# Keys in two planes: the second plane of a batch added by an accumulating transfer

## The chip, the cores and the metric

One NeuronCore of one Trainium2 chip. The metric is the device time of one execution in microseconds (us), median over runs; lower is better.

## The reference, cut to what matters

Three stages follow each other: an attention over pooled keys and values, a mixture of experts over its output, and a gated two-layer network. The change touches the first. There are 8 batches of 8 heads with 576 queries of 64 numbers, and the 576 keys are averaged in groups of 8, so 72 pooled keys are left.

```python
def _attn_ref(q, k, v):
    B, H, S, D = q.shape          # 8, 8, 576, 64
    pool = 8
    Sp = S // pool                # 72
    scale = 1.0 / np.sqrt(D)
    k_p = k.reshape(B, H, Sp, pool, D).mean(axis=3)
    v_p = v.reshape(B, H, Sp, pool, D).mean(axis=3)
    scores = scale * np.matmul(q, k_p.transpose(0, 1, 3, 2))
    scores = scores - np.max(scores, axis=-1, keepdims=True)
    attn = np.exp(scores)
    attn = attn / (np.sum(attn, axis=-1, keepdims=True) + 1e-09)
    return np.matmul(attn, v_p)
```

## The kernel before

`attention` runs over 36 tiles of 128 queries, 9 tiles for each two batches (the ninth is half of the one batch and half of the other). Each engine executes its instructions in the order in which the code issues them, except that DMA issues may be placed somewhat ahead of other work of their engine. Iteration i of the loop issues work for three tiles at once:

- `scores(i + 2)`: TensorE multiplies queries and pooled keys (`s<-kbd,q`, two PSUM tiles from the shared pool `hp` of three), VectorE takes the maxima (`mx<-s`), ScalarE the exponentials (`prb<-s,mx`, eight instructions).
- `ptrans(i + 1)`: TensorE transposes the probabilities (`pt<-ident,prb`), ScalarE copies them out of PSUM (`pts<-pt`).
- `pv(i)`: TensorE multiplies them with the pooled values (`pv<-vex,pts`); its PSUM tile has one buffer, so `pv(i + 1)` waits until VectorE's `post(i)` (`sm`, `cc`, `x`, `lg`) has read it.

Behind that, iteration i also prepares the batch b + 1 that comes next, placed by `first[b]`, the first tile of batch b (0, 4, 9, 13, 18, 22, 27, 31). For b from 1 to 6:

- at i = first[b] - 2: `loadq(b + 1)` on SyncE's queue, the first half of `pool_k(b + 1)` on VectorE, `pool_v(b + 1)` on GpSimd (`v<-v` twice, then `vp<-v`), and then `loadk(b + 2)`, `loadv(b + 2)` on SyncE's queue;
- at i = first[b] - 1: the second half of `pool_k(b + 1)`;
- at i = first[b]: `keys(b + 1)`, two ScalarE instructions that scale the pooled keys into `kbd`;
- at i = first[b] + 1: `router1(b + 1)` (TensorE `vtp<-ident,vp`, which needs `vp`) and `values(b + 1)` on GpSimd.

A half of `pool_k` is one VectorE reduction over two of the four head pairs: 128 partitions, 144 outputs, 8 numbers each. The keys of a batch are one transfer of 1152 KB (batch 0: two of 576 KB, one for each half), into a tile with two buffers.

After the ninth tile of a group, `route` appends two steps to a list; the next two iterations pop them. So the iterations i = 9, 18 and 27, which are first[b] for b = 2, 4 and 6, carry ten small VectorE instructions of routing, the iteration behind them about as many more, and GpSimd then issues nine small scatters (`slots<-consts,ix`), two to an iteration.

`raw1` and `raw2` are the landing buffers of the first expert's weights, 16 KB to a partition each; they are written from iteration 25 on.

Of the kernel before, what the change touches and what calls it, by code (L numbers as in the profile page):

```python
# [5 lines left out]
F32 = mybir.dt.float32  # L6
# [7 lines left out]
ALU = mybir.AluOpType  # L14
AX = mybir.AxisListType
# [3 lines left out]
P = 128  # L19
B, H, S, D = 8, 8, 576, 64  # L20
G = 72
# [23 lines left out]
POOL = 8  # L45
# [107 lines left out]
class Kern:  # L153
# [19 lines left out]
    def attention(self, xa, rs, extra):  # L173
        nc, tc, c = self.nc, self.tc, self.c
        self.todo = todo = []
        self.slow = iter(())
        with tc.tile_pool(name="as", bufs=1) as s1, \
# [7 lines left out]
            wr = s1.tile([P, 2, H * (E + 1)], F32, name="wr", tag="wr")  # L185
            mv = c[:, C_MV:C_MV + NINC]
            q_t, k_t, v_t, st = {}, {}, {}, {}

            def loadk(b):
                k_t[b] = s2.tile([P, 4, G, POOL], F32, name=f"k{b}", tag="k")  # L190
                nc.sync.dma_start(k_t[b].rearrange("p a g t -> p a (g t)"), self.kT[b])

            def loadv(b):
                v_t[b] = s2.tile([P, NC, POOL, D], F32, name=f"v{b}", tag="v")
# [3 lines left out]
            def loadq(b):  # L198
                q_t[b] = s2.tile([P, 4, S], F32, name=f"q{b}", tag="q", bufs=3)
                nc.sync.dma_start(q_t[b], self.qT[b])  # L200

            def pool_k(b, eng, halves=(0, 2)):
                k = k_t[b]
                kp = st.get((b, "k"))
                if kp is None:
                    kp = s2.tile([P, 4, G], F32, name=f"kp_{b}", tag="kp")
                if eng is nc.vector:
                    for a in halves:
                        eng.tensor_reduce(kp[:, a:a + 2], k[:, a:a + 2], AX.X, ALU.add)
                else:  # L210
                    eng.tensor_tensor(k[:, :, :, 0:4], k[:, :, :, 0:4], k[:, :, :, 4:8], ALU.add)
                    eng.tensor_tensor(k[:, :, :, 0:2], k[:, :, :, 0:2], k[:, :, :, 2:4], ALU.add)
                    eng.tensor_tensor(kp, k[:, :, :, 0], k[:, :, :, 1], ALU.add)
                st[b, "k"] = kp

            def pool_v(b, on_dve=0):

                v, g, n = v_t.pop(b), nc.gpsimd, on_dve
                vp = st[b, "v"] = s2.tile([P, NC, D], F32, name=f"vp_{b}", tag="vp")
                if n:  # L220
                    nc.vector.tensor_reduce(vp[:CP, 0:n], v[:CP, 0:n].rearrange("p c t d -> p c d t"), AX.X, ALU.add)
                v, vp = v[:CP, n:], vp[:CP, n:]
                g.tensor_tensor(v[:, :, 0:4], v[:, :, 0:4], v[:, :, 4:8], ALU.add)
                g.tensor_tensor(v[:, :, 0:2], v[:, :, 0:2], v[:, :, 2:4], ALU.add)
                g.tensor_tensor(vp, v[:, :, 0], v[:, :, 1], ALU.add)

            def values(b):
                vp, ve = st[b, "v"], vex[b % NB]
                for i, (h0, n) in enumerate(HEADS):
                    j = HOFF[i]  # L230
                    nc.gpsimd.tensor_tensor(ve[:CP, j:j + n, 0:D], bc(vp[:CP, i], 1, n),
                                            bc(mv[:CP, j:j + n], 2, D), ALU.mult)

            def keys(b):
                kp, kb = st.pop((b, "k")), kbd[b % NB]
                for j in range(2):
                    nc.scalar.mul(kb[:, :, j, :], kp, c[:, C_E + j:C_E + j + 1])
# [47 lines left out]
            def scores(t, pss=None):  # L285
                pss = pss or products(t)
                pr = prb[t % 2]
                mx = s2.tile([P, H], F32, name=f"mx_{t}", tag="mx")
                for a, ps in enumerate(pss):
                    nc.vector.tensor_reduce(mx[:, 4 * a:4 * a + 4],  # L290
                                            ps[:, 0:288].rearrange("p (h g) -> p h g", g=G), AX.X, ALU.max,
                                            negate=True)
                    for h in range(4):
                        nc.scalar.activation(pr[:, G * (4 * a + h):G * (4 * a + h + 1)], ps[:, G * h:G * (h + 1)],
                                             AF.Exp, bias=mx[:, 4 * a + h:4 * a + h + 1])
                return pr
# [47 lines left out]
            first = [9 * (b // 2) + 4 * (b % 2) for b in range(B)]  # L344
            one = s1.tile([1, 1], F32, name="one", tag="one")
            self.cb = s1.tile([P, C_N - C_TRI], F32, name="constb", tag="constb")
            nc.vector.memset(one, 0.0)
            k_t[0] = s2.tile([P, 4, G, POOL], F32, name="k0", tag="k")
            for a in (0, 2):
                nc.sync.dma_start(k_t[0][:, a:a + 2].rearrange("p a g t -> p a (g t)"), self.kT[0][:, a:a + 2])  # L350
            nc.scalar.dma_start(self.ident, self.con[:, 0:P])
            nc.scalar.dma_start(c, self.con[:, P:P + C_TRI])
            q_t[0] = s2.tile([P, 4, S], F32, name="q0", tag="q", bufs=3)
# [18 lines left out]
            for i in range(-2, NTILE):  # L372
                if i == -2:
                    pool_v(0, ON0)
                if i + 2 < NTILE and i != -1:
                    prs[i + 2] = scores(i + 2)
                ready = todo.pop(0) if todo and i < NTILE - 1 else None
                if ready and ready[0]:
                    ready[0]()
                if i == -2:  # L380
                    values(0)
                    loadv(1)
                    loadq(1)
                if i == -1:
                    pss = products(1)
                    router1(0)
                if i == 0:
                    pv(0, pts.pop(0))
                if 0 <= i + 1 < NTILE:
                    pts[i + 1] = ptrans(i + 1, prs.pop(i + 1))  # L390
                if i == -1:
                    prs[1] = scores(1, pss)
                    router2(0)
                    pool_k(1, nc.vector, (0,))
                    pool_v(1, ON1)
                    values(1)
                if i > 0:
                    pv(i, pts.pop(i))
                a = ready[1]() if ready and ready[1] else iter(())
                b = post(i) if i >= 0 else iter(())  # L400
                for _ in range(ready[2] if ready and i < NTILE - 2 else 0):
                    next(a, None)
                for _ in b:
                    next(a, None)
                for _ in a:
                    pass
                for _ in range(SLOW):
                    next(self.slow, None)
                if i == 0:
                    pool_k(1, nc.vector, (2,))  # L410
                    keys(1)
                for b in range(B):
                    if i + 2 == first[b]:
                        if 0 < b < B - 1:
                            loadq(b + 1)
                            pool_k(b + 1, nc.vector, (0,))
                            pool_v(b + 1)
                        if b + 2 < B:
                            loadk(b + 2)
                            loadv(b + 2)  # L420
                    if i + 2 == first[b] + 3 + (b == 0) and b + 1 < B:
                        router1(b + 1)
                    if i + 2 == first[b] + 1 and 0 < b < B - 1:
                        pool_k(b + 1, nc.vector, (2,))
                    if i + 2 == first[b] + 2 and 0 < b < B - 1:
                        keys(b + 1)
                    if i + 2 == first[b] + 3 and 0 < b < B - 1:
                        values(b + 1)
                    if i + 2 == first[b] + 5 and b + 1 < B:
                        router2(b + 1)  # L430
                if i == 2:
                    nc.sync.dma_start(self.cb, self.con[:, P + C_TRI:])
                if i == 6:
                    self.consts()
                self.place(2 if i < 27 else 5)
                extra(i)
# [1100 lines left out]
def layout(q, k, v, w_skip, w_gate):  # L1537
    def tr(a):
        return np.ascontiguousarray(a.reshape(B, 4, 2, S, D).transpose(0, 2, 4, 1, 3)).reshape(B, P, 4, S)
    vr = v.reshape(B, H * G, POOL * D)  # L1540
    vr = np.concatenate([vr, np.zeros((B, NC * CP - H * G, POOL * D), v.dtype)], 1)
    vr = vr.reshape(B, NC, CP, POOL * D).transpose(0, 2, 1, 3)
    vr = np.concatenate([vr, np.zeros((B, P - CP, NC, POOL * D), v.dtype)], 1)
    wr = np.concatenate([w_gate, w_skip[:, None]], 1).reshape(H, D, E + 1).transpose(1, 0, 2).reshape(D, H * (E + 1))
    z = np.zeros_like(wr)
    wr = np.ascontiguousarray(np.stack([np.concatenate([wr, z], 0), np.concatenate([z, wr], 0)], 1))
    return tr(q), tr(k), vr, wr


def build(tc, qT, kT, vR, wr, con, w1, w2, w_in, w_out, out):  # L1550
# [55 lines left out]
```

## Time and profile before

| | |
|---|---|
| median of 3 runs | 1301.69 us (1301.1 to 1304.04) |
| the profiled execution's own time | 1305.57 us |
| its span, first to last instruction | 1303.8 us |
| granted TensorE clock, mean over the span | 0.992 |
| busy: PE, DVE, ACT, POOL | 1253.7, 851.5, 576.1, 352.6 us |
| the attention stage | from the start to about 160 us of the span |

PE is TensorE's matmul stream, DVE is VectorE, ACT is ScalarE, POOL is GpSimd, SPq the instructions that SyncE issues to its DMA queue. A number in brackets behind a timeline row is the idle time of that engine just before it and what ended it. Times in the rows are counted from the span's start.

### The profile page before, as it was taken

To read this page: it belongs to the slowest core of one execution; us is meant where nothing else is said; L and a number is where in the kernel's file an instruction comes from. 1 tells how busy PE (TensorE), PEld (TensorE's weight loads), DVE (VectorE), ACT (ScalarE), POOL (GpSimd) and SP (SyncE) were. 2 spreads that over 40 slices of the span, in tenths; PEclk is the share of its full clock that TensorE was granted. 3 is DMA by queue.
4 is the path that set the end of the run, shared out by engine and by line. 5 is a ranking of instruction groups with operands and counts; after the bars stand their busy time and mean duration, and the time that the engine had idled before them with its cause. 6 is when DMAs were issued, how large, how long until landed. Compare 5 with 4: busy or idle time off the path is not lost.

```text
span 1303.8 us, 20308 instructions
## 1 busy us (share of the span) xinstructions
PE 1253.7 (96%) x6469; PEld 1063.6 (82%) x6470; DVE 851.5 (65%) x1557; ACT 576.1 (44%) x1224; POOL 352.6 (27%) x312
## 2 busy tenths in 40 slices
PE   6999797999989999999999999999999999999998
PEld 5888677988888878878888888788888888888887
DVE  5888685676676767879734235556784657847565
ACT  4777534444555445354433344523344343533321
POOL 5466432122222222213457503101111010211100
PEclk9999998999999998999999999999999999999999
DMA  8888446465575632448754322644446353463532
GB/s 343 291 300 284 148 135 212 168 219 189 178 237 185 220 128 91 145 163 269 264 188 183 129 89 103 212 162 137 151 172 218 124 176 111 156 213 118 178 111 91
DMA packets 94187, 234.43 MB, mean 180 GB/s; under 512 B 15077, under 2 KB 26981, under 8 KB 90400
## 3 DMA queue, kind: packets, MB, share of 16 engines
q1 hardware_dynamic: 86816, 216.47, 47.7%
q0 software_dynamic: 7008, 16.80, 4.1%
q8 instruction: 42, 0.69, 0.2%
q14 instruction: 33, 0.27, 0.1%
q10 hardware_dynamic: 288, 0.20, 0.1%
HBM read 183.24 MB, written 52.89 MB: 181 GB/s over the span
## 4 chain that ended last, share of the span: by engine, by line
PE 59%; DVE 2%; DMA 1%; issue 0%; ACT 0%; SPq 0%; DVEq 0%; ACTq 0%
PE yb L110 21%; PE ps L110 17%; PE fh L110 9%; PE fop L110 9%; PE hp L110 2%; PE yp L110 1%; DVE ft L110 1%; PE fxp L110 1%; DVE fr L110 0%; DMA wout<-wdo 0%; PE sx L110 0%; DVE fgl L110 0%; DVE fsg L110 0%; DMA out<-fo 0%; ACT fgh L110 0%
## 5 line engine op out<-in xcount | busy, mean ns | idle before, releaser
L110 PE MATMUL yb<-wout,g 128*128 128x512 f32 x1152 | 268.5, 391 | 0.5 <-DMA wout<-wdo 0.5
L110 PEld LDWEIGHTS yb<-wout,g 128*128 128x128 f32 x1152 | 215.0, 188 | 45.6 <-DMA wout<-wdo 0.7
L110 POOL TENSOR_TENSOR tm<-tm,tm 128x512 f32<-128x512 f32 x24 | 32.2, 1340 | 411.5 <-ACT tm L110 411.5
L110 DVE TENSOR_TENSOR yacc<-yb,yacc 128x512 f32<-128x512 f32 x168 | 115.9, 690 | 38.4 <-PE yb L110 31.2
L110 ACT COPY tm<-ps 128x512 f32<-128x512 f32 x72 | 42.3, 587 | 146.5 <-PE ps L110 144.7
L110 ACT CAST g<-sg 128x512 fp32r<-128x512 f32 x96 | 59.6, 621 | 76.6 <-DVE sg L110 76.6
L110 DVE TENSOR_TENSOR fsg<-fh,fsg 128x512 f32<-128x512 f32 x48 | 33.0, 688 | 81.2 <-ACT fsg L110 81.2
L110 ACT ACTIVATE hh<-hp 128x256 fp32r<-128x256 f32 (+1 forms) x96 | 39.4, 410 | 105.6 <-PE hp L110 96.1
L110 DVE TENSOR_TENSOR w2l<-raw,w2h 128x512 fp32r<-128x512 f32 x96 | 66.1, 693 | 29.2 <-ACT w2h L110 22.2
L110 ACT ACTIVATE prb<-s,mx 128x72 f32<-128x72 f32 x288 | 64.9, 344 | 43.6 <-DVE mx L110 36.7
L110 PE MATMUL yp<-w2h,hh 128*128 128x512 f32 x208 | 83.3, 401 | 0.1
L110 PE MATMUL fh<-w1l,fh 128*128 128x512 f32 x336 | 83.4, 390 | 0.0
L110 PE MATMUL yp<-w2l,hh 128*128 128x512 f32 x208 | 81.2, 390 | 2.1 <-DVE w2l L110 2.1
L110 PE MATMUL hp<-xth,w1h 128*128 128x256 f32 (+2 forms) x384 | 73.3, 314 | 10.2 <-issue 5.9
L110 PE MATMUL yp<-w2h,hl 128*128 128x512 f32 x208 | 81.4, 391 | 0.0
L110 DVE TENSOR_TENSOR tm<-ps,tm 128x512 f32<-128x512 f32 x24 | 16.6, 691 | 98.1 <-PE ps L110 98.1
L110 PE MATMUL hp<-xtl,w1h 128*128 128x256 f32 (+2 forms) x384 | 73.4, 313 | 2.8 <-DVE xtl L110 2.7
L110 PEld LDWEIGHTS fh<-w1l,fh 128*128 128x128 f32 x336 | 62.8, 188 | 12.9
L110 PE MATMUL hp<-xth,w1l 128*128 128x256 f32 (+2 forms) x384 | 71.4, 309 | 0.0
L110 PEld LDWEIGHTS hp<-xth,w1h 128*128 128x128 f32 x384 | 61.4, 195 | 12.1 <-issue 11.0
L110 DVE TENSOR_TENSOR g<-sg,g 128x512 fp32r<-128x512 f32 x96 | 65.7, 685 | 5.4 <-ACT g L110 5.0
L110 ACT ACTIVATE fsg<-fh 128x512 f32<-128x512 f32 x48 | 28.8, 599 | 90.6 <-PE fh L110 90.6
(242 smaller groups left out, 2768.2 us busy)
## 6 DMA issues: line engine op xcount, KB each, us to landing
raw<-w SPq DMA_DIRECT2D x88, 512.0 KB, 3.8
wout<-wdo SPq DMA_DIRECT2D x48, 512.0 KB
win<-wdi SPq DMA_DIRECT2D x36, 512.0 KB
w1l<-wdi SPq DMA_DIRECT2D x36, 512.0 KB
xa<-x SPq DMA_DIRECT2D x36, 256.0 KB
fx<-xa SPq DMA_DIRECT2D x9, 1024.0 KB
v<-vR SPq DMA_DIRECT2D x7, 1280.0 KB
fr<-w_in SPq DMA_DIRECT2D x16, 512.0 KB
```

What stands on the lines that cost most here:

```text
L110: ins = f(*a, **k)
```

## The change

The host lays the keys out in two planes: the first four numbers of every group of eight, and the last four. Batches 0 and 1 load both planes, into `raw1` and `raw2`, and VectorE sums over plane and number at once. From batch 2 on the first plane alone is loaded by SyncE's queue, into a tile of half the size with four buffers; GpSimd then issues a transfer that adds the second plane onto it in SBUF (`addk`), ahead of `pool_v`, and VectorE sums four numbers. Both halves of `pool_k(b + 1)` now stand at i = first[b], just ahead of `keys(b + 1)`.

```diff
             def loadk(b):
-                k_t[b] = s2.tile([P, 4, G, POOL], F32, name=f"k{b}", tag="k")
-                nc.sync.dma_start(k_t[b].rearrange("p a g t -> p a (g t)"), self.kT[b])
+                if b < 2:
+                    raw = (self.raw1, self.raw2)[b].rearrange("p a n -> p (a n)")
+                    k_t[b] = raw[:, 0:POOL * 4 * G].rearrange("p (h a g t) -> p h a g t", h=2, a=4, g=G)
+                else:
+                    k_t[b] = s2.tile([P, 1, 4, G, POOL // 2], F32, name=f"k{b}", tag="k", bufs=4)
+                for h in range(2 if b < 2 else 1):
+                    nc.sync.dma_start(half(b, h), self.kT[b, h])
+
+            def half(b, h=0):
+                return k_t[b][:, h].rearrange("p a g t -> p (a g t)")
+
+            def addk(b):
+                nc.gpsimd.dma_start(half(b), self.kT[b, 1], accum_op=ALU.add)
...
-                if eng is nc.vector:
-                    for a in halves:
-                        eng.tensor_reduce(kp[:, a:a + 2], k[:, a:a + 2], AX.X, ALU.add)
-                else:
...
+                for a in halves:
+                    if b < 2:
+                        eng.tensor_reduce(kp[:, a:a + 2], k[:, :, a:a + 2].rearrange("p h a g t -> p a g h t"), AX.XY,
+                                          ALU.add)
+                    else:
+                        eng.tensor_reduce(kp[:, a:a + 2], k[:, 0, a:a + 2], AX.X, ALU.add)
...
-            k_t[0] = s2.tile([P, 4, G, POOL], F32, name="k0", tag="k")
-            for a in (0, 2):
-                nc.sync.dma_start(k_t[0][:, a:a + 2].rearrange("p a g t -> p a (g t)"), self.kT[0][:, a:a + 2])
+            loadk(0)
...
                     if i + 2 == first[b]:
                         if 0 < b < B - 1:
                             loadq(b + 1)
-                            pool_k(b + 1, nc.vector, (0,))
+                            addk(b + 1)
                             pool_v(b + 1)
...
-                    if i + 2 == first[b] + 1 and 0 < b < B - 1:
-                        pool_k(b + 1, nc.vector, (2,))
                     if i + 2 == first[b] + 2 and 0 < b < B - 1:
+                        pool_k(b + 1, nc.vector)
                         keys(b + 1)
```

## Rows read from the trace of the kernel before

**Rows 1.** The page: busy us of the engines, share of the span, instructions.
```profile
PE 1253.7 (96%) x6469; PEld 1063.6 (82%) x6470; DVE 851.5 (65%) x1557; ACT 576.1 (44%) x1224; POOL 352.6 (27%) x312
```

**Rows 2.** Busy time by stretches of 20 us, the sum of 20 to 140 us.
```profile
sum 120.00, PE 111.68 PEld 100.14 DVE 94.91 ACT 85.71 POOL 76.96; mean PE 18.61 PEld 16.69 DVE 15.82 ACT 14.29 POOL 12.83
```

**Rows 3.** The tile k: its reductions, shortest, median and longest in ns.
```profile
L110 DVE TENSOR_REDUCE kp<-k x16: 1339/1342/1353, 4.8 to 121.4; 128x144 f32<-128x1152 f32 x16
```

**Rows 4.** Timeline (start, length, engine), batch 4 being prepared, 64 to 78 us.
```profile
64.97 1.35 DVE L110 TENSOR_REDUCE kp<-k 128x144 f32<-128x1152 f32 x1
...
66.71 1.80 ACT L110 ACTIVATE prb<-s,mx 128x72 f32<-128x72 f32 x8 [2.04 <-DVE mx L110]
...
67.72 1.60 PE L110 MATMUL s<-kbd,q 128*128 128x144 f32 x8 [0.16 <-ACT prb L110]
...
69.70 1.55 PE L110 MATMUL pv<-vex,pts 120*128 120x148 f32 x10
...
71.09 1.16 PE L110 MATMUL s<-kbd,q 128*128 128x144 f32 x8
...
72.48 0.27 DVE L110 TENSOR_REDUCE lg<-cc 128x9 f32<-128x72 f32 x1
...
72.71 0.76 PE L110 MATMUL pt<-ident,prb 128*120 128x128 f32 x5 [0.46 <-ACT prb L110]
72.75 1.04 ACT L110 ACTIVATE kbd<-kp,consts 128x288 f32<-128x288 f32 x2
...
73.61 1.86 ACT L110 ACTIVATE prb<-s,mx 128x72 f32<-128x72 f32 x8
...
75.10 1.25 PE L110 MATMUL s<-kbd,q 128*64 128x144 f32 x16
...
76.88 1.55 PE L110 MATMUL pv<-vex,pts 120*128 120x148 f32 x10
```

**Rows 5.** Groups of VectorE by form, 20 to 140 us: busy us, mean ns.
```profile
L110 DVE TENSOR_REDUCE mx<-s 128x4 f32<-128x288 f32 x62 | 25.1, 447 | 0.1
```

**Rows 6.** Timeline of the start, 6 to 14 us.
```profile
6.63 1.35 DVE L110 TENSOR_REDUCE kp<-k 128x144 f32<-128x1152 f32 x1 [0.51 <-DMA k<-kT]
...
9.03 2.29 PE L110 MATMUL s<-kbd,q 128*128 128x144 f32 x8 [9.03 <-ACT kbd L110]
9.42 2.78 DVE L110 TENSOR_REDUCE vp<-v 120x192 f32<-120x1536 f32 x1 [1.44 <-DMA v<-vR]
...
13.19 2.29 PE L110 MATMUL s<-kbd,q 128*128 128x144 f32 x8 [1.86 <-DMA q<-qT]
```

**Rows 7.** Timelines of VectorE and TensorE, batch 5 being prepared, 86 to 98 us.
```profile
87.14 1.34 DVE L110 TENSOR_REDUCE kp<-k 128x144 f32<-128x1152 f32 x1
...
92.05 0.82 DVE L110 TENSOR_REDUCE mx<-s 128x4 f32<-128x288 f32 x2
...
92.10 1.63 PE L110 MATMUL pv<-vex,pts 120*128 120x148 f32 x10 [0.23 <-DVE x L110]
...
96.19 1.63 PE L110 MATMUL pv<-vex,pts 120*128 120x148 f32 x10 [0.50 <-DVE sel L110]
```

**Rows 8.** Timelines of GpSimd and TensorE: a direct DMA issue, pooling of batch 4.
```profile
8.78 0.79 POOL L110 DMA_DIRECT2D slots<-table  x1 [0.21 <-POOL x L110]
...
63.43 0.98 POOL L110 DMA_INDIRECT slots<-consts,ix  x1 [0.30 <-issue]
...
72.53 0.87 POOL L110 TENSOR_TENSOR vp<-v 120x320 f32<-120x320 f32 x1
...
74.70 0.47 PE L110 MATMUL vtp<-ident,vp 120*128 120x120 f32 x3
```

**Rows 9.** DMA: GB/s in 40 slices of 20 to 140 us, an issue, a load's landing.
```profile
GB/s 421 431 358 48 313 418 397 322 170 79 323 421 407 283 113 235 381 418 360 188 90 235 421 423 326 186 115 304 422 360 338 133 128 319 352 384 307 350 387 24
...
65.30 0.38 SPq L110 DMA_DIRECT2D q<-qT  x1
...
raw<-w SPq DMA_DIRECT2D x88, 512.0 KB, 3.8
```

More of the change, by code (lines that the diff above doesn't have):

```diff
@@ L206, in pool_k @@
                     kp = s2.tile([P, 4, G], F32, name=f"kp_{b}", tag="kp")
-                if eng is nc.vector:
-                    for a in halves:
-                        eng.tensor_reduce(kp[:, a:a + 2], k[:, a:a + 2], AX.X, ALU.add)
-                else:
-                    eng.tensor_tensor(k[:, :, :, 0:4], k[:, :, :, 0:4], k[:, :, :, 4:8], ALU.add)
-                    eng.tensor_tensor(k[:, :, :, 0:2], k[:, :, :, 0:2], k[:, :, :, 2:4], ALU.add)
-                    eng.tensor_tensor(kp, k[:, :, :, 0], k[:, :, :, 1], ALU.add)
+                for a in halves:
[4 more added lines that the diff above has]
+                        eng.tensor_reduce(kp[:, a:a + 2], k[:, 0, a:a + 2], AX.X, ALU.add)
                 st[b, "k"] = kp
@@ L1543, in layout @@
     vr = np.concatenate([vr, np.zeros((B, P - CP, NC, POOL * D), v.dtype)], 1)
+    kt = np.ascontiguousarray(tr(k).reshape(B, P, 4, G, 2, POOL // 2).transpose(0, 4, 1, 2, 3, 5)).reshape(B, 2, P, -1)
     wr = np.concatenate([w_gate, w_skip[:, None]], 1).reshape(H, D, E + 1).transpose(1, 0, 2).reshape(D, H * (E + 1))
@@ L1546, in layout @@
     wr = np.ascontiguousarray(np.stack([np.concatenate([wr, z], 0), np.concatenate([z, wr], 0)], 1))
-    return tr(q), tr(k), vr, wr
+    return tr(q), kt, vr, wr
 def build(tc, qT, kT, vR, wr, con, w1, w2, w_in, w_out, out):
```

## Prediction

> **What bounds the kernel now.** First the page: TensorE's stream is busy for 96% of the span [rows 1], so work taken from another engine helps only where TensorE stood waiting for it. Then the stretches of the stage that changes: from 20 to 140 us TensorE is busy 111.7 of 120 us, VectorE 94.9, ScalarE 85.7 [rows 2]. All that TensorE could win there is 8.3 us, 0.6% of the kernel. Then the tile k: 16 reductions of 1.34 us [rows 3], 12 of which (batches 2 to 7) the change shortens. Last the timeline around them, for what a reduction holds up; this decides.
>
> Take batch 4. The reduction at 64.97 stands in VectorE's queue ahead of the maxima of tile 14; ScalarE idles 2.04 us for those, its exponentials start at 66.71, and TensorE, which needs their PSUM tiles back, runs its next products in 1.60 instead of about 1.15 us (as at 71.09) after waiting 0.16 [rows 4]. The second one, an iteration later, does the same to tile 15: the transposes at 72.71 had waited 0.46 us [rows 4]. So a reduction of 1.34 us costs TensorE about 0.6 us; it comes twice in each of six batches. That is the prize, about 7 us at most.
>
> **What the reductions become.** The trace has none of 576 elements. Between the row for 288 elements (447 ns) [rows 5] and the one for 1152 (1342 ns) [rows 3] a line gives 447 + 288 x 895/864 = 745 ns. The next instruction starts 1.26 us after a reduction recorded at 1.35 (64.97 to 66.23), so I count 0.66 us each, 1.33 for the pair. Bounds: half of 1342, 0.67, and 576 at the rate of the strided sum over v, 2783 ns for 1536 elements [rows 6], 1.04. On VectorE 12 x (1.26 - 0.66) = 7.2 us go away. But the pair is now issued in one iteration, and directly ahead of keys.
>
> **Batches 2, 4 and 6** (no routing in that iteration), worked on batch 4. Without the early reductions the exponentials of tile 14 start 1.26 earlier, at about 65.5, the products of tile 15 follow the work before them at 67.56, where the wait of 0.16 began, and take 1.15, and pv(13) starts at 69.1 instead of 69.70. The second one gone, the transposes at 72.71 lose their wait too: pv(14) at 72.1 instead of 73.31. So far 1.2 us won. Now the cost: post(13) ended at 72.48 + 0.27 [rows 4] and ends 0.6 earlier, at 72.1; the pair runs until 73.45; keys waits for it on ScalarE and takes 0.95 (before, it ran at 72.75, in front of the exponentials but waiting for nothing [rows 4]); the exponentials of tile 16, queued behind keys, start at 74.4 instead of 73.61. TensorE's products at 75.10 started 1.49 after those, being in need of their PSUM tiles, so now 75.9, and pv(15), 1.78 behind, at 77.7 instead of 76.88 [rows 4]. Two stalls of 0.6 become one of 2.0, because reductions, keys and exponentials now stand in one chain. Net +0.8 us for the batch, +2.4 for three, which repeat the pattern.
>
> **Batches 3, 5 and 7** share that iteration with routing. VectorE has no gap from the reduction at 87.14 to behind the maxima at 92.05, and pv(19) and pv(20) wait for VectorE (0.23 and 0.50) [rows 7]. Taking 1.26 out at 87.14 and putting 1.33 in behind post(18) brings pv(19) from 92.10 to about 90.85, but the maxima at 92.05 come where they came, as does all behind them up to pv(20) at 96.19. Keys pushes the exponentials back 0.5 us, beside VectorE's backlog. I count 0 for the three; bounds -0.6 and +0.5 each.
>
> **The start.** Both planes of batch 0 are needed at once. The second transfer of k was there at 6.63 [rows 6]; both reductions now start there and end at 9.3 instead of 7.98, so the first products move from 9.03 to 10.4 and end at 12.7. The products of tile 1 start at 13.19, waiting for queries [rows 6]: the delay is covered, 0. If summing over two planes ran at the strided rate of v, 2.09 us each, the first products would end at 14.1: +1.0, and +0.6 for batch 1's two reductions at 0.4 of their extra 0.75. So 0 to +1.6; I take 0, since four contiguous numbers are nearer to rows 3 than a stride at every element.
>
> **GpSimd's issue.** A direct issue took 0.79 us [rows 8]. Tightest is batch 4, where pool_v stands behind four scatters: vp ended at 73.40, TensorE read it at 74.70 [rows 8], a slack of 1.3 us. In the new chain TensorE would wait at that place until 75.9 anyway. So 0; an issue beyond 2 us would show there.
>
> **The accumulating transfer** is in no row. VectorE needs it at 72.1 for batch 4. The third of GpSimd's four scatters starts at 63.43 and takes 0.98, with 0.30 before each [rows 8]; the transfer stands behind the second or the fourth, so it is issued at 63.4 or by 66.7. SyncE's queue issues q, k and v from 65.30 on, and such a burst fills the next slices at 381 to 418 GB/s [rows 9]. Lower end: it lands like a plain load of 512 KB, 3.8 us after its issue [rows 9], at 70.5; at 420 GB/s 1.25 of that are bytes and 2.5 are not. Upper end: behind the whole burst (3008 KB) and itself counted twice, since it must read what it adds to: 4.26 MB at 420 GB/s, 10.1 us, and 2.5: 79.3, 7.2 late. Sharing evenly with the burst, as two queues would, it takes 2.8 us counted once and 5.6 twice, landing at 72.0 or 74.8. I take on time, the plain load being the nearest row. Batch 6 has the same crowding; for batches 2, 3, 5 and 7 no scatters stand ahead of it, and GpSimd comes to it well before SyncE's burst of that iteration or after its end.
>
> The Trainium skill, page DMA: Bandwidth & Descriptors, section Issuing engines are not separate DMA queues, says that transfers issued from GpSimd run on the same 16 DMA engines as SyncE's and interleave with them. No row can show that for this transfer; by that rule the even share above holds, not the free landing. Its page Collectives: The Full Stack, section on the bandwidth ceiling, puts a reducing transfer at half the rate of a copy, for its two source reads. By both together this transfer lands at 74.8 for batches 4 and 6, and the sum would be +7.8.
>
> **The sum.** 3 x 0.8 + 3 x 0 + 0 + 0 + 0 = +2.4 us. The profiled execution took 1305.57 us, 1.77 around its span of 1303.8, so 1308.0 for the like of it; it lies 3.9 above the median of 1301.69, against which I give **1304.1 us**, +0.18%. About 0.2%, 2.6 us, is what a measurement of this kernel can tell from no change.
>
> **Rivals.**
> 1. *The sum comes late* (slower). If the accumulating transfers of batches 4 and 6 land at 74.8, counted twice and shared evenly, VectorE stands at the pair for 2.7 us, with the maxima and post behind it in its queue, ScalarE behind those and TensorE behind both: +2.4 + 2 x 2.7 = +7.8, 1309.5. For it: SyncE's burst is issued within 1.4 us of it. Against: scatters are placed ahead of pool_v's sums, and the issue may be too, at 63.4, into a slice of 113 GB/s. It decides from a landing 5.4 us after the issue on. At its upper end 1318.5.
> 2. *The stalls come back whole* (faster). If keys finds room and the pair is absorbed, batches 2, 4 and 6 keep their 1.2 us each: -3.6, 1298.1. For it: ScalarE idles up to 2 us an iteration. Against: keys directly precedes the exponentials in its queue, and TensorE started 1.49 us after those began.
> 3. *The two-plane sums are slow* (slower): +1.6 at the start, 1305.7.
> 4. The change not doing what it says is the case of the pair at 1.04 us each: VectorE is relieved of little, and 0.75 us more go onto each of six chains: +4.5 on top, 1308.6.
>
> **Chances.** Forecast 0.45, late sum 0.20, stalls back 0.22, slow start or slow pair 0.13. The forecast's own range is 1301 to 1306; a third of it lies above the 2.6. From these: faster 0.22 (nearly all of the second rival and a little of the forecast), same 0.38, slower 0.40. The range runs from the second rival to just past the first: 1298 to 1310.
>
> **What would show it.** 12 reductions at about 745 ns, directly behind lg at the tiles 4, 9, 13, 18, 22 and 27; keys idle until they end; the products behind them later; the second products at the start still waiting for q at about 13.2. A wait of VectorE for the transfer of k at batches 4 or 6 shows the first rival, pv(15) earlier than 76.88 by a microsecond the second, reductions of batches 0 and 1 above 1.4 us the third. The end of the attention stage should move by about as much as the whole; where the total moves without it, my reading of where this change acts is wrong.

## The result, and the profile after

The changed kernel takes 1310.05 us (median of 4 runs, 1309.76 to 1310.63), the kernel before 1301.91 on the same chip: ratio 1.0055, 95% interval 1.0039 to 1.0071, so it is slower by 5 to 9 us. The forecast was 1304.1, slower too, but by 2.4 us where 7.1 came (0.55%, the ratio; between the two medians lie 8.1); the time lies at the very end of the range. The profiled execution is that of 1310.63 us, its span 1308.9.

First the rows that answer to [rows 1 to 3]: the page's busy times, the sum of the windows from 20 to 140 us, and the tile k (shortest, median, longest in ns).

```profile
PE 1253.6 (96%) x6469; PEld 1062.5 (81%) x6470; DVE 842.8 (64%) x1557; ACT 575.8 (44%) x1224; POOL 360.0 (28%) x318
...
sum 120.00, PE 109.13 PEld 98.03 DVE 86.26 ACT 84.39 POOL 82.10; mean PE 18.19 PEld 16.34 DVE 14.38 ACT 14.06 POOL 13.68
...
L110 DVE TENSOR_REDUCE kp<-k x12: 741/742/744, 37.7 to 127.4; 128x144 f32<-128x576 f32 x12
L110 POOL DMA_DIRECT2D k<-kT x6: 892/1016/1025, 27.5 to 115.0; - x6
```

A reduction takes 742 ns, VectorE is relieved by 8.7 us over the span, and TensorE does 2.6 us less work in those 120 us than before: it stood longer. Next the timeline of batch 4 in the changed kernel, beside [rows 4].

```profile
69.41 1.55 PE L110 MATMUL pv<-vex,pts 120*128 120x148 f32 x10
...
72.18 0.27 DVE L110 TENSOR_REDUCE lg<-cc 128x9 f32<-128x72 f32 x1
72.37 1.40 DVE L110 TENSOR_REDUCE kp<-k 128x144 f32<-128x576 f32 x2
...
72.41 1.63 PE L110 MATMUL pv<-vex,pts 120*128 120x148 f32 x10
73.69 0.81 DVE L110 TENSOR_REDUCE mx<-s 128x4 f32<-128x288 f32 x2
...
73.81 0.96 ACT L110 ACTIVATE kbd<-kp,consts 128x288 f32<-128x288 f32 x2 [2.13 <-DVE kp L110]
73.88 0.47 PE L110 MATMUL vtp<-ident,vp 120*128 120x120 f32 x3
...
74.68 1.78 ACT L110 ACTIVATE prb<-s,mx 128x72 f32<-128x72 f32 x8
...
75.66 1.56 PE L110 MATMUL s<-kbd,q 128*64 128x144 f32 x16 [1.32 <-ACT prb L110]
...
77.75 1.43 PE L110 MATMUL pv<-vex,pts 120*128 120x148 f32 x9
```

That is the chain of the prediction: pair, keys (ScalarE idle 2.13 us for it), exponentials, products for which TensorE stood 1.32 us, pv(15) at 77.75 where 77.7 was forecast. VectorE starts the pair right behind lg and waits for no transfer.

So the place where the change acts looks as expected, and the time is lost elsewhere. The starts of pv in TensorE's timelines say where (tiles down; e1 and e5 are second profiles of the two kernels, e9, e3 and e7 experiments below; e1 and e3 ran on chip 5, e5 and e7 on chip 12, e9 on chip 10, and for "before" and "after" the chip is not on record):

```
tile  before      e1   after      e5      e9      e3      e7
   3   31.21   31.43   30.70   30.87   30.97   30.26   31.25
   6   42.85   43.07   43.08   43.26   43.35   42.63   42.89
  12   65.05   65.29   65.36   65.53   65.62   64.91   65.83
  15   76.88   76.98   77.75   77.94   78.00   77.30   77.70
  21   99.49   99.59  100.42  100.61  100.65   99.97  100.31
  24  111.14  111.23  112.80  112.99  113.03  112.35  111.95
  29  130.29  130.37  131.99  132.18  132.22  132.74  131.14
  31  140.73  138.91  145.79  146.16  140.67  141.19  145.18
  35  159.83  159.08  165.07  164.78  160.42  161.14  164.24
```

Read a column against "before". The changed kernel begins 0.51 us ahead, and up to tile 29, behind the last batch's keys, it has become 1.70 us behind: 2.2 us for the six batches. Between tiles 29 and 31 it loses 3.4 us more (5.3 against e1), where no instruction of the change stands. A second loss is at the start of the feed-forward part. Here ScalarE's activation fsg, and TensorE's product that needs it, in the changed kernel (timelines of the two engines):

```profile
570.86 0.60 ACT L110 ACTIVATE fsg<-fh 128x512 f32<-128x512 f32 x1 [5.27 <-PE fh L110]
...
572.89 0.50 PE L110 MATMUL fop<-fh,fgh 128*128 128x512 f32 x1 [2.48 <-ACT fgh L110]
```

and the same activation in the kernel before (e1):

```profile
561.47 0.60 ACT L110 ACTIVATE fsg<-fh 128x512 f32<-128x512 f32 x1 [2.20 <-PE fh L110]
```

ScalarE idles 5.27 instead of 2.20 us ahead of it: 3 us during which its input lay ready.

### The profile page after: what moved, and what is told of

It is laid out like the page before. It is cut to its first block, busy times and chain, and to the rows that moved or that the text cites. A ratio compares the mean times of both kernels' runs of the same rounds, so it can differ in the third digit from the quotient of the medians.

```text
span 1308.9 us, 20326 instructions
## 1 busy us (share of the span) xinstructions
PE 1253.6 (96%) x6469; PEld 1062.5 (81%) x6470; DVE 842.8 (64%) x1557; ACT 575.8 (44%) x1224; POOL 360.0 (28%) x318
## 4 chain that ended last, share of the span: by engine, by line
PE 57%; DVE 3%; ACT 1%; issue 1%; POOL 0%; DMA 0%; DVEq 0%; ACTq 0%; POOLq 0%
PE yb L110 20%; PE ps L110 17%; PE fop L110 9%; PE fh L110 9%; PE yp L110 1%; DVE fr L110 1%; DVE ft L110 1%; PE fxp L110 1%; DVE raw L110 0%; DVE fsg L110 0%; PE sx L110 0%; DVE fgl L110 0%; DVE w2l L110 0%; ACT g L110 0%; PE hp L110 0%
## 5 line engine op out<-in xcount | busy, mean ns | idle before, releaser
L110 PE MATMUL fop<-fh,fgh 128*128 128x512 f32 x168 | 67.1, 400 | 2.5 <-ACT fgh L110 2.5
```

Of the source, the lines that this page charges most:

```text
L110: ins = f(*a, **k)
```

## The experiments

Each ratio is against the kernel before on the same chip. e1 to e4 ran on chip 5, e5 to e8 on chip 12, e9 to e12 on chip 10; the medians of the kernel before there are 1299.03, 1303.50 and 1299.18 us (1301.91 beside the result). The changed kernel itself ran beside the result and on chip 12, never on 5 or 10. Profiles of different chips are set side by side below, and for the stall between the tiles 29 and 31 that matters, as will be seen.

**e1, the kernel before again.** No edit.

> The kernel before, unchanged, for a second profile of it. Its first profiled execution (1305.57 us) lay 3.9 above the median. If that is usual for a profiled execution, this one takes 1304 to 1307 and the tiles 29 to 31 come at the same places as in the first profile (within 0.5 us). If the first one was an odd one, this takes about 1302, and the difference to the changed kernel's profile is 8 us, to be looked for again.

1299.83 us, beside a median of 1299.03. Up to tile 29 both profiles agree within 0.25 us; at tile 31 the first one is 1.8 later. So the profile that the prediction was read from held a stall of its own. e1 holds none and is what the others are compared with, but it is a profile of chip 5.

**e2, second plane moved but not added.**

```diff
-                nc.gpsimd.dma_start(half(b), self.kT[b, 1], accum_op=ALU.add)
+                spare = s2.tile([P, 4 * G * POOL // 2], F32, name=f"spare{b}", tag="spare", bufs=1)
+                nc.gpsimd.dma_start(spare, self.kT[b, 1])
```

The tile of the first plane also has three buffers instead of four, which makes room for the other one.

> The changed kernel, but the second plane of batches 2 to 7 goes by a plain transfer, from the same queue at the same place, into a tile of its own that nobody reads; it is left out of the sums of the keys. Bytes, issues, order and VectorE's work stay. Theory 'transfer' (the accumulating transfer holds the 16 DMA engines twice as long per byte, and at the end of the stage, where the weights load and the engines are 99% busy, that delays the others): the 3.4 us between tiles 29 and 31 go, 1305 to 1307. Theory 'chain' (the pair, the keys and the exponentials one behind the other, and whatever the later end of batch 7's keys does to the end of the stage): nothing changes, 1309 to 1311.

With half of each key left out the router sends tokens to other experts, so the whole (1319.01 us) says nothing here; only the attention stage is read. It came as "transfer" expected: 2.4 us behind e1 at tile 29, 2.4 at tile 31, no stall between. But no profile of chip 5 has that stall, and the changed kernel was not run there, so this doesn't tell the theories apart. The stretch from 20 to 140 us also prices the accumulation (DMA view, queues: packets, MB, share of 16 engines). The changed kernel:

```profile
q1 hardware_dynamic: 12307, 31.41, 70.6%
q0 software_dynamic: 1624, 3.55, 17.9%
```

and e2:

```profile
q1 hardware_dynamic: 12296, 31.35, 74.1%
q0 software_dynamic: 1592, 3.55, 10.3%
```

The same 3.55 MB hold the engines 1.74 times as long when they are added. Packet by packet, 4608 bytes take 366 to 493 ns (means of the six transfers) with the addition, 221 to 316 without.

**e3, batch 7 by plain transfers.**

```diff
+                elif b == B - 1:
+                    k_t[b] = s1.tile([P, 2, 4, G, POOL // 2], F32, name="k7", tag="k7")
...
-                            addk(b + 1)
+                            if b + 1 < B - 1:
+                                addk(b + 1)
```

Batch 7's two reductions then sum over two planes, and the other batches' key tile has two buffers instead of four.

> The changed kernel, but batch 7's keys come as two plain transfers, an early one each, and its two reductions sum over two planes (1.34 us each again, still in one iteration). Theory 'transfer': batch 7's accumulating transfer is the one that runs beside the weights, so most of the 3.4 us go and 0.6 to 1.2 come in for the longer pair: 1307 to 1308.5. Theory 'chain': a longer pair at batch 7 makes it worse, 1310.5 to 1312.

1306.93 us, 1.0060 (1.0047 to 1.0074). The stall between 29 and 31 is absent (2.37 behind e1 at 29, 2.28 at 31), as "transfer" said, but it is absent from every profile of this chip; and in ratio the whole is as slow as the changed kernel. The stall of the feed-forward part is here too (ScalarE idle 5.26): TensorE is 2.7 us behind e1 ahead of it and 7.1 behind it.

**e4, halves apart, transfer earlier.**

```diff
+                    if i + 2 == first[b] - 2 and 0 < b < B - 1:
+                        addk(b + 1)
+                    if i + 2 == first[b] + 1 and 0 < b < B - 1:
+                        pool_k(b + 1, nc.vector, (2,))
...
-                            addk(b + 1)
+                            pool_k(b + 1, nc.vector, (0,))
...
-                        pool_k(b + 1, nc.vector)
                         keys(b + 1)
```

> The changed kernel, but the accumulating transfer is issued two iterations earlier and the two short reductions stand where the reductions of the kernel before stood, one and two iterations ahead of the keys. Theory 'chain': the three chains of +0.8 turn into stalls of 0.3 instead of 0.6 us (six batches, two each, 3 us in all below before's stage), and with batch 7's keys early the end of the stage comes right too: 1300 to 1304. Theory 'transfer': only the 2.4 us of the chain and the 1 to 3 of shorter stalls are won, the end of the stage still loses its 3.4: 1304.5 to 1307.

1304.40 us, 1.0046 (1.0032 to 1.0060). Both theories missed, because the first rival came true: VectorE waited for the transfer. Its waits from 20 to 140 us (us in total, times, longest):

```profile
DVE kp L110 <- DMA k<-kT: 7.9, 4, 2.8
```

The tiles behind the three long ones came 2.7, 2.7 and 2.3 us later (against e1), while batches 3, 4 and 6, on time, gained 0.6, 0.8 and 0.7. There was no stall between 29 and 31, nor in the feed-forward part, although batch 7's transfer was issued only 5.5 us ahead of the weights (5.8 in the changed kernel). On this chip that speaks neither for "transfer" nor against it.

**e5, the changed kernel again.** No edit.

> The changed kernel, unchanged, on one chip with the three others. Its first profile holds two stalls that the second profile of the kernel before lacks: 5 us between the tiles 29 and 31 of the attention stage, and 2.9 us at the start of the feed-forward part, far from the change. If both belong to the kernel, they stand here too and the ratio is 1.005 to 1.007. If they come and go, the end of the stage lies 1.5 us or more elsewhere than in the first profile.

1310.37 us, 1.0054 (1.0041 to 1.0067). Both stalls are there again: tile 31 lies 7.25 us behind e1 (6.88 in the first profile), and ScalarE idles 5.27 us ahead of fsg. The second is in every kernel with as many ScalarE instructions, on three chips (table below). The first came both times; whether the kernel or the chip makes it is taken up below.

**e6, transfer one iteration earlier.** e4 with `first[b] - 3`.

> As e4_halves_apart, but the accumulating transfer is issued one iteration earlier still. In e4 VectorE waited for it three times (2.2, 2.7 and 2.8 us), and the tiles behind those waits came 2.7, 2.7 and 2.0 us later. Theory 'late sum' (e4 lost by those waits alone): they go, the stage ends 1 to 3 us ahead of that of the kernel before, ratio 0.997 to 1.000. Theory 'occupancy' (what counts is the DMA engines' longer occupation, wherever the transfer stands): the stage ends 1 to 4 us behind it, ratio 1.001 to 1.004.

1306.66 us, 1.0026 (1.0013 to 1.0038). It missed its aim: GpSimd, whose queue is in order, now stood waiting for the first plane to land (17.8 us, twice), and VectorE still waited 8.1 us in four places, up to 3.9. This tells nothing of occupancy. The stall between tiles 30 and 31 is there (2.9 us), the other one is not.

**e7, only batch 7 as in the changed kernel.**

```diff
-                            addk(b + 1)
+                            if b + 1 < B - 1:
+                                pool_k(b + 1, nc.vector, (0,))
+                            else:
+                                addk(b + 1)
...
+                    if i + 2 == first[b] + 1 and 0 < b < B - 2:
+                        pool_k(b + 1, nc.vector, (2,))
                     if i + 2 == first[b] + 2 and 0 < b < B - 1:
-                        pool_k(b + 1, nc.vector)
+                        if b + 1 == B - 1:
+                            pool_k(b + 1, nc.vector)
```

> The kernel before in its order, with two planes: batches 2 to 6 come by plain transfers and are summed where the kernel before summed them, 1.34 us a half; batch 7 alone is changed as in the changed kernel (accumulating transfer, short pair right ahead of the keys). Theory 'transfer at the end' (batch 7's accumulating transfer, issued just ahead of the first expert's weights, makes the 3.4 us): as before up to tile 27 (within 0.6 us), then 4 to 6 us behind at tile 31, ratio 1.003 to 1.005. Theory 'chain' (the late keys alone): 1.3 us behind at tile 31, ratio 1.000 to 1.0015.

1306.58 us, 1.0026 (1.0016 to 1.0036): below what "transfer" gave, above "chain". In the profile, 0.8 us behind e1 at tile 29 and 6.3 at tile 31: batch 7's part alone comes with the whole stall. How much of it the kernel before has on this chip is not known, as it has no profile there.

**e8, second half of the weights later.**

```diff
-                if i in (25, 27):
+                if i in (25, 31):
```

> The changed kernel, but the second of the first expert's weights (2 MB) is loaded four iterations later, at 31 instead of 27; nothing in the attention stage reads it. Theory 'transfer at the end': with half of the competing bytes gone from 128 to 138 us, at least 2 of the 3.4 us between tiles 29 and 31 go, 1306 to 1308 for 1310, ratio 1.003 to 1.004. Theory 'chain': no change, 1.0055. If the weights are then late for the expert's part, the time is lost there instead, and the stage's end tells the two apart.

1309.15 us, 1.0046 (1.0032 to 1.0060). 1.9 us behind e1 at tile 29, 4.6 at 31 (7.25 in e5): the stall shrinks by 2.6. Both are of chip 12, one profile each: with fewer bytes moving beside it the stall is smaller. The feed-forward stall stands.

**e9, one more instruction on ScalarE.** By now the feed-forward stall had a pattern that no theory about DMA explained. It stood where ScalarE's compiled program has 1402 instructions.

```diff
             nc.scalar.activation(one, one, AF.Exp)
+            nc.scalar.copy(one, one)
```

> The changed kernel with one copy of a single number more on ScalarE, at the very start, where it is idle. Why: the stall of 2.8 to 3.2 us at the start of the feed-forward part stood in the five profiles of kernels whose ScalarE program has 1402 instructions (the changed one twice, e2, e3, e8) and in none of those with 1397 (before, twice), 1399 (e7) or 1403 (e4, e6). Theory 'position' (it hangs on where that place lies in ScalarE's program): the stall goes, 2 to 4 us less than the changed kernel, ratio 1.002 to 1.004. Theory 'load' (it comes from what the accumulating transfers or the later end of attention leave behind): it stays, 1.0055.

1299.17 us (12 runs), 1.0000 (0.9991 to 1.0010). One copy of one number more, and the feed-forward stall is gone; in its profile ScalarE idles 2.20 us ahead of fsg, as before. "Position" had expected 3 us back, and 7 came. They can't all be put down to the copy: the stall between the tiles 29 and 31 is absent too, as from every profile of chip 10, and the changed kernel without the copy was not run there. What the copy alone is worth, e12 tells beside e3. The row of fsg:

```profile
563.25 0.60 ACT L110 ACTIVATE fsg<-fh 128x512 f32<-128x512 f32 x1 [2.20 <-PE fh L110]
```

**e10, five more in the kernel before.** The same line five times in the kernel before.

> The kernel before with five such copies more on ScalarE at the very start, 1402 instructions as in the changed kernel. Theory 'position', if the count alone sets the place: the stall of 3 us at the start of the feed-forward part appears here, ratio 1.002 to 1.003. Theory 'load': nothing changes, 0.999 to 1.001.

1304.25 us, 1.0037 (1.0024 to 1.0050). The stall appears in a kernel without any of the change, on the same chip as the runs that it is compared with; it is 4.8 us slower where about 3 were expected:

```profile
564.88 0.60 ACT L110 ACTIVATE fsg<-fh 128x512 f32<-128x512 f32 x1 [5.28 <-PE fh L110]
```

**e11, three batches.** e4, but only for batches 3, 4 and 6; the others with two plain planes and the reductions of before.

```diff
+ADD = (3, 4, 6)
...
-                            addk(b + 1)
+                            pool_k(b + 1, nc.vector, (0,))
...
+                        if b + 1 in ADD:
+                            addk(b + 1)
```

> Only batches 3, 4 and 6 are added onto by an accumulating transfer, issued as in e4, where VectorE did not wait for these three; their short halves stand where the kernel before had its reductions. Batches 2, 5 and 7 come as two plain planes and are summed where the kernel before sums them. ScalarE's program has 1401 instructions. If a half of 0.74 in place of 1.34 us is worth what e4 shows at these batches (0.6, 0.9 and 0.6 us), the stage ends 1.5 to 2.5 us ahead of the kernel before and the ratio is 0.998 to 1.000. If the longer occupation of the DMA engines takes that back, 1.000 to 1.003.

1299.78 us, 1.0004 (0.9995 to 1.0013). The stage did what was expected, ending 2.1 us ahead of e1; 1.4 us went again in the feed-forward part, where in this kernel the cast behind fsg comes late. With ScalarE's program shifted it might gain 0.1%; that was not tried.

**e12, both suspects out.** e3 with the copy of e9.

> Both found causes taken out of the changed kernel: batch 7's keys come plainly as in e3, and ScalarE has one copy more at the start as in e9. If they are the whole of what the prediction missed, its sum is left: the stage ends 2 to 2.5 us behind the kernel before, no stall at the start of the feed-forward part, ratio 1.001 to 1.003 (e3 had 1.006). If the ratio stays at 1.004 or above, something else is missing.

1303.02 us, 1.0026 (1.0015 to 1.0037), in the expected band, and without the feed-forward stall. e3, the same kernel without the copy, had 1.0060 on chip 5: by these two ratios the copy is worth 4.4 us. The stage ends 2.36 us behind e1. The profile shows other halts, though: 2.2 us at the transposes vtp of batch 7, where TensorE's queue waited for nothing that is shown, and some 3 us in pieces between 190 and 226, of which 1 comes back.

## Why the prediction was right in its steps and wrong in its sum

**Right: what the instructions of the change cost.** The reductions: 742 ns for 745 forecast, 1.40 us recorded for a pair. Batches 2, 4 and 6: 0.74, 0.56 and 0.73 us for 0.8 each (column "after" less "before", tiles 3 to 6, 12 to 15, 21 to 24). Batches 3, 5 and 7: 0.08, 0.06 and 0.04 for 0. Together 2.2 for 2.4. Against e1, e9 gives 2.3, and there the figures are 0.74, 0.05, 0.69, 0.04, 0.74 and 0.05. The mechanism holds too: in batch 4, pv(14) has won 1.2 us on tile 12, as forecast, and pv(15) then loses 1.8 for 2.0.

**Right: the start.** The first products moved from 9.03 [rows 6] to 10.85 (10.4 forecast; the sums began at 7.19 instead of 6.63, when the second plane was there), and the second ones still waited for queries:

```profile
10.85 2.29 PE L110 MATMUL s<-kbd,q 128*128 128x144 f32 x8 [10.85 <-ACT kbd L110]
...
13.64 2.29 PE L110 MATMUL s<-kbd,q 128*128 128x144 f32 x8 [0.50 <-DMA q<-qT]
```

Tile 0 then came 0.52 earlier. That is no gain of the change: e10, with none of it, begins 1.0 us ahead of e1.

**Right: GpSimd's issue and the transfer on time.** An issue takes 1.02 us for 0.79 [rows 8], and vtp at 73.88 waits for nothing. Batch 4's transfer was issued at 63.45, its last packet ended at 69.23, VectorE wanted it at 72.37; over the six batches the last packet ended 5.6 to 8.6 us after the issue. The page Collectives: The Full Stack of the Trainium skill, section on the bandwidth ceiling, lets the reducing transfers of a collective run at half a copy's rate; this case's transfer took 1.74 times as long as a plain one, nearly that. What made the first rival false was the time: batch 4's transfer was issued at the earlier of the two places that the prediction left open (63.4 or 66.7) and met few other bytes (0.15 MB from other queues while it ran). e4 shows the price where it is late, 2.2 to 2.8 us each, close to the 2.7 that the rival had.

**False: the other rivals.** Batches 2, 4 and 6 lost their 0.56 to 0.74 (second), two-plane sums took 1344 ns (third), and the pair 0.70 us a half (fourth).

**The step that failed** is the last one: "The sum. 3 x 0.8 + 3 x 0 + 0 + 0 + 0", taken for the whole, with "the end of the attention stage should move by about as much as the whole". It priced the instructions of the change and gave everything else a silent zero. That zero was wrong by 4.7 us (7.1 measured, 2.4 forecast). In the profiles, TensorE of the changed kernel is 1.6 us behind e1 at tile 29, 6.0 at tile 35, 6.3 ahead of the feed-forward stall and 10.7 behind it, from there to the end; in e5 it is 1.8, 5.7, 6.2 and 9.0. So nearly all that was missed lies in two places. e9 shows that the change's own work doesn't cost it: the same change with one more instruction on ScalarE, on a chip without the other stall, is level with the kernel before, within 1.3 us. (Its stage ends 1.3 us behind e1, having been 1.9 behind at tile 29; the 2.4 of the forecast doesn't show in its whole either, and no run tells where it goes.) That the measured time still lies in the range is luck: the range reached up to 1310 for the first rival, a late transfer, which did not happen. The two parts of the zero:

*The feed-forward stall, 3 us of ScalarE and 2.8 to 4.4 of TensorE, shown.* The DMA view has a queue of kind instruction, number 14, which brings pieces of 8 KB:

```profile
q14 instruction: 34, 0.28, 0.1%
```

When single packets of it start, and which instruction of ScalarE follows, in the feed-forward part (ScalarE's program in instructions; us):

```
kernel  program   packet   follows             after it
e1         1397   565.08   cast fgh at 567.55      2.48
after      1402   569.34   fsg at 570.86           1.52
e5         1402   569.25   fsg at 570.76           1.51
e2         1402   577.95   fsg at 579.47           1.52
e3         1402   565.76   fsg at 567.27           1.51
e8         1402   567.73   fsg at 569.25           1.52
e10        1402   563.36   fsg at 564.88           1.52
e11        1401   561.62   cast fgh at 563.14      1.52
e7         1399   571.52   next fsg at 573.22      1.70
e9         1403   553.31   busy, no wait              -
```

In the six profiles with 1402 instructions ScalarE starts fsg 1.51 to 1.52 us behind the packet, whether the change is in the kernel or not; one instruction fewer, and the wait falls on the next one; with 1397 the packet falls where ScalarE waits for VectorE anyway (2.77 us ahead of that fgh in e1, 2.76 in e9). So ScalarE had run out of program there. Two things are less sure: other engines' pieces come on this queue too, so that the packet is ScalarE's is read from the times; and with 1403 instructions (e4, e6, e9, e12) it comes some nine instructions earlier, not one, while ScalarE has work. The page Runtime: NRT & Kernel Launch of the Trainium skill (Terms) says that an engine's instruction memory is refilled in blocks, of 16 KiB; the trace agrees on the refilling, and on this queue shows 8 KB. The change adds five instructions to ScalarE's program (1397 to 1402), waits that come with the new order, and so put the border of a piece on an activation that TensorE needs at once.

TensorE loses more than its idle time of 2.48 us. These are its products ahead of the stall and behind it, in e1:

```profile
558.48 1.98 PE L110 MATMUL fh<-w1l,fh 128*128 128x512 f32 x8
...
566.65 2.88 PE L110 MATMUL fh<-w1l,w1h 128*128 128x512 f32 x12
```

and in the changed kernel:

```profile
564.81 1.98 PE L110 MATMUL fh<-w1l,fh 128*128 128x512 f32 x8
...
577.35 2.91 PE L110 MATMUL fh<-w1l,w1h 128*128 128x512 f32 x12
```

It was 6.3 us behind and is 10.7 behind: 4.4 lost. After the idle time its granted clock was 0.51 for 3.4 us, the lower of its two levels (1.2 for 2.4 GHz), and it did 9 products there; in e5, after the same idle time, it stayed at 1.00, with 17 products and 2.8 us lost. The two rows of the windows view (length, then busy time and count of PE, PEld, DVE, ACT and POOL; the number 0.51 or 1.00 is the clock), the changed kernel first:

```profile
573.40:576.80 3.40, 3.40 (x9) 2.69 (x9) 3.37 (x4) 0.00 (x0) 0.00 (x0) 0.51 0.00 0
```

```profile
573.40:576.80 3.40, 3.40 (x17) 2.79 (x16) 3.37 (x5) 0.00 (x0) 0.00 (x0) 1.00 0.00 0
```

e3, e8 and e10 have the low clock too and lose 4.1 to 4.3 us. That fits the whole runs, 4.8 us in e10 and 4.4 between e3 and e12. In e7 the border costs ScalarE 2.5 us and TensorE nothing.

*The stall between tiles 29 and 31, 3.4 us more than in "before" and 5.3 or 5.4 more than in e1, open in its cause.* My theory was the accumulating transfer of batch 7 beside the weights; e2, e3, e7 and e8 came as it said, e4 and e9 did not. But the chip sorts the profiles better than the transfer does. Against e1, all six of the result's session and of chip 12 have the stall (before 1.9 us, after 5.3, e5 5.4, e6 2.9, e7 5.5, e8 2.8), and none of the eight of chips 5 and 10, among them e4 and e9 with that transfer. So the transfer can't be the cause by itself, e2 and e3 don't speak for it, and that one more instruction on ScalarE avoids the stall is not shown. Among the six, the kernel before has the least those with batch 7's transfer where the changed kernel has it and all of the weights beside it have the most (after, e5, e7), and with half of the weights later (e8) or the transfer earlier (e6) about half of that is left. So where there is a stall, the transfer beside the weights seems to make it longer, by one profile of each kernel; the changed kernel on chip 5 or 10, and a profile of the kernel before on chip 12, would tell. What the stall looks like is shown by pv(29) and the instruction of VectorE that needs it, in e5 (chip 12; timelines of TensorE and VectorE):

```profile
132.18 1.55 PE L110 MATMUL pv<-vex,pts 120*128 120x148 f32 x10
...
135.37 0.17 DVE L110 TENSOR_SCALAR sm<-pv 128x8 f32<-128x8 f32 x1 [2.51 <-PE pt L110]
...
136.78 1.63 PE L110 MATMUL pv<-vex,pts 120*128 120x148 f32 x10 [1.26 <-PE pt L110]
...
144.14 0.17 DVE L110 TENSOR_SCALAR sm<-pv 128x8 f32<-128x8 f32 x1 [3.25 <-PE pt L110]
```

and in e9 (chip 10):

```profile
132.22 1.55 PE L110 MATMUL pv<-vex,pts 120*128 120x148 f32 x10
...
133.81 0.17 DVE L110 TENSOR_SCALAR sm<-pv 128x8 f32<-128x8 f32 x1 [0.90 <-PE pv L110]
```

pv(29) ends at 133.7 or 133.8 in both; VectorE goes on 0.04 us later in e9 and 1.6 in e5. pv(30) ends at 138.4 in e5, and VectorE takes it up 5.7 later, the last 3.25 of them idle. The semaphore which TensorE raises for it, as its updates are recorded between 132.3 and 145.2 us:

```
e9  132.39 133.78 134.28 134.77 135.35 135.57 136.96 137.89 139.46 140.30 140.63 140.85 141.10 ... 144.56
e5  132.36 135.34 136.80 140.40 142.56 144.00 144.11 144.19 144.25 144.31 144.36 145.15
```

In e5 few come for 12 us, then six within 0.4. Records are missing there: of this semaphore e5's whole trace has 830, e9's 851. That goes with the stall as well as the chip does: 826 to 833 records in the six profiles that have it, 849 to 851 in the eight that don't. Whether the recording takes part in the stall, or something else makes both, no run told. The late starts stand in VectorE's own rows all the same, and the kernel before is slower in the session and on the chip that have them (1301.91 and 1303.50 us for 1299.03 and 1299.18). The DMA engines are full in this stretch with the stall and without (0.99 busy from 120 to 140 us in the changed kernel and in e9).

## What to carry to other kernels

Work out the change's own instructions, then compare the same tiles in both traces: where the loss begins at a tile that the change doesn't touch, look for a cause that isn't the change. Before a difference under 1% is put down to an edit, run it once more with an instruction added where its engine idles at the start, and the kernel before too; here that was worth 4.4 us between e3 and e12 and 4.8 in the kernel before, more than the edit. Do it on one chip, with a profile of both kernels there: a stall of up to 5.5 us was in every profile of one chip and in none of another, and that passed for an effect of four experiments. The accumulating transfer cost nothing where it was issued early and met little else, and 2.2 to 2.8 us of waiting each time where it came late (e4).

## What the runs showed of the hardware

A border in ScalarE's program cost 1.7 to 3.1 us where ScalarE reached it with nothing left to do (idle 5.27 instead of 2.20 us with 1402 instructions, 2.48 for 0.76 with 1401, 3.28 for 0.74 with 1399). Between 1399 and 1402 it moved by one instruction for each that was added ahead of it; at 1403 it moved further. Behind the same idle time of 2.48 us TensorE's granted clock fell to 0.51 in the changed kernel and stayed at 1.00 in e5. An accumulating transfer into SBUF held the DMA engines 1.74 times as long as a plain one of the same 3.55 MB (one profile each, e2 for the plain one). And TensorE's semaphore updates came late by some us in profiles that also lost records: its work had ended at 133.7 us, VectorE learned of it at 135.4.
